# Halving the first batch's queries and giving every user of PSUM one bank, in an attention kernel followed by two matrix products

## The chip, the cores and the metric

The kernel runs on one core of one Trainium2 chip. The metric is the device time of one execution in microseconds (us), smaller is better. All executions quoted here are in the fast state, but for one of `e7_scores_apart`, which is left out of its figures. The medians are of the executions named beside them; an interval is a 95% interval of a ratio.

The engines are PE (the matmul engine, whose weight loads are listed apart as PEld), DVE and ACT (vector and scalar engine), POOL (permuting copies, and it issues the loads), SP (it issues transposes and stores) and 16 shared DMA engines. PSUM is the memory to which PE writes its results; it is handed out in banks. In these traces the engines keep to the program's order: two profiles of the changed kernel (the one below and `a0_changed_again`) have the same sequence on PE, DVE, ACT and POOL, 3584 matmuls on PE, though their waits differ by microseconds.

## The reference

```python
# q, k, v: (8, 12, 448, 64): batch, heads, sequence, head size
scores = q @ k.T / 8
e = exp(scores - max)
attn = (e / (sum(e) + exp(-max))) @ v              # "softmax off by one"
x = attn, heads side by side                       # (8*448, 768)
h = x @ w_in                                       # (3584, 2048)
g = (a0 + a1 h + a2 h^2 + a3 h^3) / (1 + |b0||h| + |b1|h^2 + 1e-6)
out = g @ w_out                                    # (3584, 768), float32
```

Below, "score pass" is a group of matmuls `k.q` and the exponential that ACT makes of it; "sums" are the softmax denominators (d) and the weighted values (u) of one unit of four heads; "products" are the matmuls of `x @ w_in`; "outputs" are those of `g @ w_out`. There are 8 batches of 3 units.

## The kernel before

The kernel is built by a small list scheduler: each operation has an engine, an estimated duration and dependencies, and a greedy loop decides in which order the engines get them. Only that order reaches the chip. Batch 0's q and k are transposed by PE, all others by DMA transposes, after POOL has permuted them into a single buffer (`qp`, `kp`):

```python
kp = ring("kp", 1, [P, 2, J, 2, D])
qt = ring("qt", NK, [128, 2, J, P])                # NK = 3; P = 112
sps = [ps.tile([128, 2, 512], F32, ...) for i in range(2)]   # scores, 2 x 2 PSUM banks
gen = [ps.tile([128, 2, 512], F32, ...) for i in range(2)]   # all others, 2 x 2 banks
# ... cut ...
            pm = plan.add("perm", Op(f"pm{name}{n}", "POOL", 1.1, [ld[n], hist(xps, n, 1)], ...))
            x = plan.add("x", Op(f"x{name}{n}", "SP", 0.1, [pm, hist(qk_free, n, NK)], emit_x))
# ... cut: emit_x is nc.sync.dma_start_transpose(out=qt[...], in_=qp[...]) ...
        if b == 0:
            transpose_by_pe(n)
        else:
            transpose_by_dma(n)
```

A unit's sums are queued between the next unit's score passes, in two portions; after batch 0's last unit they stand alone:

```python
    for n in range(NB):
        beats = attention(n)                       # 8 score passes
        for half in range(2):
            for s in beats[2 * half:2 * half + 2]:
                plan.add("att", s)
            if prev is not None:
                plan.add("att", prev[half])        # d, then u, of the unit before
        for s in beats[4:]:
            plan.add("att", s)
        prev = attend(n)
        if n == NQ - 1 or n == NB - 1:             # NQ = 3
            for op in prev:
                plan.add("att", op)
            prev = None
```

The products of two column blocks of 128 fill one double slot of `gen` and leave it by one cast 896 wide:

```python
                for c in range(f % 2 * NQ, f % 2 * NQ + NQ):
                    nc.tensor.matmul(out=gen[unit["slot"]][:, f // 2, 0:S],
                                     lhsT=w_in_sb[gi][...], rhs=x_sb[b % NX][:, c, :], ...)
```

The loads go out in this order: keys, queries and values of units 0 to 2, `w_in0`, unit 3, `w_in1`, `w_in2`, unit 4, `w_in3`, unit 5, `w_out0` to `w_out3`, then the later units.

The softmax here doesn't subtract the row's maximum and nothing guards it: scores larger than these inputs give would overflow.

## Time and profile before

| | before |
|---|---|
| median of the first three runs | 482.59 us (480.96 to 482.86) |
| span of the profiled run | 479.5 us |
| PE busy, by the page | 433.8 us (90%) |
| PE streaming, by count | 392 us (82%) |
| DVE busy, ACT busy | 335.0, 319.8 us |

"Streaming" is the measure that this document argues with. A busy PE is not a streaming PE: the same product matmul has a mean of 357 ns in the groups of the page, though 24 of them in a row pass in 4.65 us (0.194 us each) in the chain of waits. So I counted the matmuls that start in each 20 us and multiplied by what one costs in an undisturbed row: 0.194 us a product, 0.163 an output, 0.051 a sum, 0.10 a score matmul; one of half length counts half. The Trainium skill ("Perfetto Trace Analysis", Identifying the Most-Contended Engine) says likewise that the busy share of matmuls is not a good measure of how close a kernel is to its limit, because they are pipelined. It expects pipelined matmuls to look smaller in the trace; here they look larger (357 for 194 ns).

The page of the kernel before: its busy times, then the span in 40 slices of 12 us, one digit a slice in tenths, then the granted PE clock and the DMA engines.

```profile
span 479.5 us, 7892 instructions
PE 433.8 (90%) x3296; PEld 210.0 (44%) x3296; DVE 335.0 (70%) x389; ACT 319.8 (67%) x337; POOL 123.0 (26%) x186
PE   3873977897998999999999999999999999998985
DVE  1210579579796887738879976766879887899900
PEclk9997889799999999999999999999999999999999
DMA  9999998915685565528777537627031011111222
```

DVE is nearly idle in the first four slices (48 us): it has no products to cast. DMA stands at 8 or 9 tenths in the first eight. PE's waits lie in the same stretch. The timeline of PE of the kernel before, as start, duration, instructions, and in brackets the wait just before them and what ended it:

```profile
35.75 1.87 PE L417 MATMUL gen<-e,vn 112*32 112x448 f16 x32
...
45.68 1.00 PE L391 MATMUL sps<-qt,kt 64*112 64x448 f16 x4 [8.05 <-DMA qt<-qp]
46.61 1.30 PE L481 MATMUL gen<-x,w_in 128*128 128x448 f16 x3
...
63.60 0.58 PE L391 MATMUL sps<-qt,kt 64*112 64x448 f16 x4 [2.98 <-DMA qt<-qp]
...
457.13 11.87 PE L569 MATMUL gen<-w_out,g 128*128 128x384 f16 x72 [1.55 <-DVE g L519]
```

Batch 0's last sums end at 37.6 us. PE stands 8.05 us before the scores of batch 1, whose queries are still in a DMA transpose, and starts the first product only at 46.61 us. The chain of waits of the kernel before (start, duration, what ran) holds these transfers:

```profile
19.53 10.13 DMA w_in<-in_moe_w_in_dram
31.42 10.43 DMA kt<-kp
46.46 17.00 DMA qt<-qp
```

A transposition of queries takes 17.00 us here. The list of DMA issues gives, last on the line, the median over the whole run:

```profile
kt<-kp SPq DMA_TRANSPOSE x21, 3.4
qt<-qp SPq DMA_TRANSPOSE x21, 3.5
```

So one and the same transpose lands three to five times later in the head, beside the weight loads, than in steady state. The form-by-form groups of the kernel before (busy us, mean ns) show two costs that the change touches, the loading of keys into PE and the casts:

```profile
L391 PEld LDWEIGHTS <-kt 64*112 64x112 f16 x384 | 21.2, 130 | 62.8 <-issue 56.4 <-DMA kt<-kp 5.8 <-DVE kt L319 0.3
L498 DVE CAST h<-gen 128x896 f16<-128x896 f32 x60 | 64.9, 1086 | 49.5 <-PE gen L481 48.8 <-issue 0.3
```

### The profile page before, as it was taken

How to read it: one execution, taken by the hardware profiler on the slowest of the kernel's cores; microseconds unless marked ns; L12 is line 12 of the kernel's file. 1: busy time of each engine (PE TensorE's matmuls, PEld its weight loads, DVE VectorE, ACT ScalarE, POOL GpSimd, SP SyncE). 2: the span in 40 equal slices, each digit the busy share in tenths (PEclk: the TensorE clock that was granted, in tenths of full speed). 3: DMA queues.
4: the chain of work that ended last, by engine and by line, in shares of the span. 5: the costliest groups of instructions: out<-in, count | busy, mean ns of one | idle time of the engine just before them, and what ended most of it. 6: DMA issues, size and time to landing. Idle time of an engine off the chain costs nothing.

```text
span 479.5 us, 7892 instructions
## 1 busy us (share of the span) xinstructions
PE 433.8 (90%) x3296; PEld 210.0 (44%) x3296; DVE 335.0 (70%) x389; ACT 319.8 (67%) x337; POOL 123.0 (26%) x186
## 2 busy tenths in 40 slices
PE   3873977897998999999999999999999999998985
PEld 2421423343543444444444444444444445554553
DVE  1210579579796887738879976766879887899900
ACT  3792477867688586966869776876679782555611
POOL 6674135504540344033430432022000100010000
PEclk9997889799999999999999999999999999999999
DMA  9999998915685565528777537627031011111222
GB/s 127 183 202 190 202 163 120 128 24 87 95 99 108 91 96 98 103 32 119 116 125 109 77 78 126 105 58 101 31 72 35 0 34 34 33 34 33 68 66 67
DMA packets 82564, 43.98 MB, mean 92 GB/s; under 512 B 41568, under 2 KB 78944, under 8 KB 82528
## 3 DMA queue, kind: packets, MB, share of 16 engines
q0 software_dynamic: 38784, 22.81, 35.3%
q1 hardware_dynamic: 43744, 20.66, 20.9%
q8 instruction: 26, 0.43, 0.4%
q14 instruction: 10, 0.08, 0.1%
HBM read 45.62 MB, written 11.01 MB: 118 GB/s over the span
## 4 chain that ended last, share of the span: by engine, by line
PE 58%; DVE 15%; ACT 11%; DMA 10%; issue 4%; POOL 1%; DVEq 0%; POOLq 0%; ACTq 0%
PE gen L569 24%; PE gen L481 19%; PE gen L417 8%; PE sps L391 6%; ACT e L397 5%; DMA w_in<-in_moe_w_in_dram 4%; DMA qt<-qp 4%; DVE h L498 3%; DVE g L519 3%; DVE n L515 2%; ACT c L533 2%; DMA kt<-kp 2%; DVE n L519 2%; DVE c L519 2%; ACT c L530 1%
## 5 line engine op out<-in xcount | busy, mean ns | idle before, releaser
L397 ACT ACTIVATE e<-sps 112x896 f16<-112x896 f32 x192 | 166.5, 922 | 83.5 <-PE sps L391 82.9
L481 PE MATMUL gen<-x,w_in 128*128 128x448 f16 x768 | 161.3, 357 | 3.8 <-ACT o L579 1.5
L569 PE MATMUL gen<-w_out,g 128*128 128x384 f16 x768 | 134.2, 326 | 2.7 <-DVE g L519 2.3
L481 PEld LDWEIGHTS <-w_in 128*128 128x128 f16 x768 | 71.3, 98 | 83.4 <-issue 25.4
L498 DVE CAST h<-gen 128x896 f16<-128x896 f32 x60 | 64.9, 1086 | 49.5 <-PE gen L481 48.8
L569 PEld LDWEIGHTS <-g 128*128 128x128 f16 x768 | 72.2, 98 | 60.9 <-issue 12.0
L391 PE MATMUL sps<-qt,kt 64*112 64x448 f16 x384 | 65.0, 395 | 21.2 <-DMA qt<-qp 11.0
L530 ACT ACTIVATE c<-c,oneeps_c 128x1792 f16<-128x1792 f16 x32 | 57.4, 1794 | 36.2 <-DVE c L519 36.1
L519 DVE TENSOR_TENSOR n<-n,h 128x1792 f16<-128x1792 f16 x64 | 71.0, 1110 | 0.9
L552 POOL COPY gx<-g 128x1024 f16<-128x1024 f16 x8 | 9.3, 1158 | 198.2 <-DVE g L519 179.2
L533 ACT ACTIVATE c<-c 128x1792 f16<-128x1792 f16 x32 | 54.5, 1702 | 0.3
L438 DVE TENSOR_TENSOR x<-gen,lden 128x896 f16<-128x896 f32 x24 | 26.1, 1086 | 35.7 <-PE gen L417 35.7
L345 POOL COPY kp<-kn 112x256 uint32<-112x256 uint32 x42 | 24.8, 620 | 101.1 <-DMA kt<-kp 96.3
L519 DVE TENSOR_TENSOR g<-n,c 128x1792 f16<-128x1792 f16 x32 | 35.0, 1095 | 21.2 <-ACT c L533 20.5
L391 PEld LDWEIGHTS <-kt 64*112 64x112 f16 x384 | 21.2, 130 | 62.8 <-issue 56.4
L515 DVE TENSOR_SCALAR n<-n,abc 128x1792 f16<-128x1792 f16 x64 | 45.2, 706 | 1.2
L417 PE MATMUL gen<-e,vn 112*32 112x448 f16 x768 | 43.1, 368 | 1.0 <-ACT lden L430 0.9
L579 ACT ACTIVATE o<-gen 128x768 f32<-128x768 f32 x28 | 22.7, 810 | 25.6 <-PE gen L569 25.6
L519 DVE TENSOR_TENSOR c<-c,w 128x1792 f16<-128x1792 f16 x32 | 35.2, 1100 | 0.0
L345 POOL COPY qp<-qn 112x256 uint32<-112x256 uint32 x42 | 27.6, 686 | 14.7 <-DMA qt<-qp 12.2
L417 PEld LDWEIGHTS <-vn 112*32 112x32 f16 x768 | 20.0, 99 | 21.6 <-issue 11.0
L417 PE MATMUL gen<-e,ones 112*32 112x448 f16 x384 | 24.9, 379 | 3.6 <-DVE h L498 3.2
(32 smaller groups left out, 230.7 us busy)
## 6 DMA issues: line engine op xcount, KB each, us to landing
kn<-in_k_dram POOLq DMA_DIRECT2D x24, 224.0 KB, 4.2
qn<-in_q_dram POOLq DMA_DIRECT2D x24, 224.0 KB, 5.0
vn<-in_v_dram POOLq DMA_DIRECT2D x24, 224.0 KB, 6.2
w_in<-in_moe_w_in_dram POOLq DMA_DIRECT2D x12, 256.0 KB, 10.1
w_out<-in_moe_w_out_dram POOLq DMA_DIRECT2D x4, 768.0 KB, 20.1
out_dram<-o SPq DMA_DIRECT2D x8, 336.0 KB, 3.0
out_dram<-o SPq DMA_DIRECT2D x8, 288.0 KB, 2.8
out_dram<-o SPq DMA_DIRECT2D x8, 240.0 KB, 2.6
```

The costliest lines, as they stand in the source:

```text
L345: nc.gpsimd.tensor_copy(out=mid[0].bitcast(U32)[:, pr], in_=src[n % NN].bitcast(U32)[:, 2 * pr:2 * pr + 2] .rearrange("p e j d -> p j e d"))
L391: nc.tensor.matmul(out=sps[m % NS][0:P, hh, 0:S], lhsT=kt[n % NK][r, pr, j, :], rhs=qt[n % NK][r, pr].rearrange("p j c -> p (j c)"), start ...
L397: nc.scalar.activation(out=e_sb[m % NE], in_=sps[m % NS][0:P, :, 0:S], func=AF.Exp, scale=scale)
L417: nc.tensor.matmul(out=gen[unit["slot"]][32 * i:32 * i + 32, half, 0:S], lhsT=lhs(i, j), rhs=e_sb[m % NE][:, i % 2, :], start=(j == 0), st ...
L438: nc.vector.tensor_tensor(out=x_sb[b % NX][:, 2 * qd:2 * qd + 2, :], in0=gen[un_u["slot"]][:, :, 0:S], in1=r, op=ALU.mult)
L481: nc.tensor.matmul(out=gen[unit["slot"]][:, f // 2, 0:S], lhsT=w_in_sb[gi][:, c // 2, c % 2, (fc % FG) * 128:(fc % FG + 1) * 128], rhs=x_s ...
L498: nc.vector.tensor_copy(out=dst, in_=src)
L515: return lambda: nc.vector.tensor_scalar(out=out, in0=in0, scalar1=s1, scalar2=s2, op0=op0, **kw)
L519: return lambda: nc.vector.tensor_tensor(out=out, in0=in0, in1=in1, op=ALU.mult)
L530: lambda: nc.scalar.activation(out=c, in_=c, func=AF.Ln, bias=oneeps_c)))
L533: lambda: nc.scalar.activation(out=c, in_=c, func=AF.Exp, scale=-1.0)))
L569: nc.tensor.matmul(out=gen[unit["slot"]][:, nh, 0:HD], lhsT=lhs, rhs=w_out_sb[f // 2][:, fc % FG, nh * HD:(nh + 1) * HD], start=(fc == 0), ...
```

## The change

The intent has four parts and a consequence.

1. *Halves.* Batch 0's attention runs for 224 query columns first and for the other 224 after. The products of the first half can start when half of the exponentials are made.
2. *Single banks.* The four banks of `gen` are handed out singly. A cast is 448 wide instead of 896, so a bank comes free sooner; casts, multiplications and output copies double in number.
3. *Joining.* A unit's sums (d and both u) are queued in one block behind the first two score passes of the next unit. The scheduler opens a unit only when three banks are free.
4. *Padding.* The keys' buffer is 16 columns longer and 128 columns are loaded as weights.
5. The queue of POOL is reordered: permutations go ahead of loads, `w_in1` ahead of unit 3, and with that `w_out1` to `w_out3` end up behind a permutation.

The diff holds more than this intent: one more buffer each for transposed q and k (NK) and for `h` (NH), and other durations and tie-breaks in the scheduler. In what follows they belong to "the other parts".

The core of the diff, with cuts:

```diff
-    NE, NX, NV, NN, NK, NH, NO, NS = 12, 3, 5, 2, 3, 2, 3, 2
+    NE, NX, NV, NN, NK, NH, NO, NS = 12, 3, 5, 2, 4, 3, 3, 2
-    qt = ring("qt", NK, [128, 2, J, P])
-    kt = ring("kt", NK, [128, 2, J, P])
+    qt = ring("qt", NK, [128, 2 * S])
+    kt = ring("kt", NK, [128, 2 * S + 16])
-    gen = [ps.tile([128, 2, 512], F32, name=f"gen{i}") for i in range(2)]
+    NGEN = 4
+    gen = [ps.tile([128, 512], F32, name=f"gen{i}") for i in range(NGEN)]
-        "POOL": ("load",  "perm", "gx"),
+        "POOL": ("perm", "load", "gx"),
+    units = [(0, qd, q0, S // 2) for q0 in (0, S // 2) for qd in range(NQ)]
+    units += [(b, qd, 0, S) for b in range(1, B) for qd in range(NQ)]
 # ... cut: in the scheduler
+            if name in ("att", "e"):
+                late = op.due > t
+                if op.opens:
+                    banks = self.bank_times()
+                    late |= len(banks) < 3 or banks[1][0] > t or banks[2][0] > t + 1.2
+                if late:
+                    rank = 9
 # ... cut: a score pass
-                            out=sps[m % NS][0:P, hh, 0:S], lhsT=kt[n % NK][r, pr, j, :],
+                                out=sps[m % NS][:, hh, ci * qw:(ci + 1) * qw],
+                                lhsT=kt[n % NK][r, c0:c0 + 128],
 # ... cut: a product and its cast
-            src = gen[unit["slot"]][:, :, 0:S]
+            src = gen[unit["bank"]][:, 0:S]
 # ... cut: the loads
-    w_in_ops = [w_in_op(0)]
+    w_in_ops = [w_in_op(0), w_in_op(1)]
     loads(3)
-    w_in_ops.append(w_in_op(1))
     w_in_ops.append(w_in_op(2))
 # ... cut: the attention queue
+    for i in range(len(units)):
+        passes = scores(i)
+        for s in passes[:2]:
+            plan.add("att", s)
+        for op in prev or []:
+            plan.add("att", op)
+        for s in passes[2:]:
+            plan.add("att", s)
+        prev = attend(i, m0)
 # ... cut: the products
+    for un in range(8):
+        slots.append((un, gemm1, (0, 0, S // 2, un)))
+        slots.append((8 + un, gemm1, (0, S // 2, S // 2, un)))
```

## The prediction

> **What bounds the kernel now.** Busy time (page, part 1): PE 434 of 479.5 us, DVE 335, ACT 320. Real streaming: the chain of waits shows 24 product matmuls in 4.65 us, 20 output matmuls in 3.36, 32 attention matmuls in 1.63, two of a score pass in 0.20. That is 0.194, 0.163, 0.051 and 0.10 us each; over 768, 896, 1152 and 384 of them about 396 us, so 84 are lost. Matmuls counted in 20 us stretches say where: 0 to 120 us holds 65 us of streaming (loss 55); 120 to 460 holds 319 of 340 (loss 21); after 460 about 5.
>
> The head: the chain runs through w_in DMAs (11.6 to 29.7 us), the first transposed keys (kt, 31.4 to 41.8) and queries (qt, 46.5 to 63.5). Such a transpose lands in 3.5 us in steady state (DMA view); here it takes 10 to 17 beside weight loads. PE, in order, stands before these scores, starts products only at 46.6 us, and is cold (granted 0.54 in 40 to 50). DVE's first cast comes at 52 us; then DVE holds PE back (100% busy at 80 to 90): two double slots serve all users.
>
> **What the change does.**
> - Batch 0 in query halves: products need half as many exponentials. At 0.81 us each, the first half's x is ready near 25 us; products fill the second half's ACT-bound attention, and DVE starts about 20 us earlier. Cost: 288 more, shorter matmuls, perhaps 2 us.
> - DMA order: w_out1 to w_out3 move behind the second permutation pair; w_in1 moves ahead of batch 1's first loads. I expect the first kt/qt at 38 and 42 us (before 41.8, 45.7), the second qt near 50 (63.5), the third near 62 (70.6).
> - Four single banks: DVE casts 60 to 120, multiplications 24 to 54, output copies 28 to 56. A 896-wide cast repeats each 1.00 us[...]: DVE +6 us, ACT +5; neither bounds. A bank frees after about 0.55 instead of 1.0 us.
> - PE block switches: 277 before, 306 after by instruction order; at about 0.1 us, +3 us. Score weights 64x112 load in 123 ns, 128-wide ones in 98 (medians). The Trainium skill ("TensorE: Matmul & The Clock Gate", Weight-path perf modes) says fast load needs 128 columns; the trace agrees in direction. Mostly hidden: at most 3 us gained.
>
> **Critical path and time.** By 65 us I expect 45 us of streaming done, a point before reached near 93. Remaining 353 us, with 4% loss (6% before; banks free sooner, a third h buffer) 14 us; tail 5; timed minus span 3. Sum 65+353+14+5+3 = 440.
>
> Predicted **441 us, range 430 to 456** (before 482.6). Chances: faster by over 2% 0.95, within 2% 0.04, slower 0.01. The gain is nearly all in the first 120 us.
>
> **What would show it.** First product matmul near 25 us (46.6); first cast near 27 (52); streaming in 0 to 120 us of 85 to 95; clock near 1.0 in 40 to 60; PE waiting for kt/qt under 10 us (17 before); from 120 us on, 19.2 or more per 20 us; kt weight loads near 98 ns; DVE 341 to 345, ACT about 325.
>
> **What would make it wrong.** If DMA, saturated to 63 us, still lands batch 1's transposes late, PE idles at 30 to 60 and half the head gain goes (455). If attention, taking three of four banks at once, starves the products, or in-order DVE and ACT delay short casts, the steady loss stays 6% or more (450). If it nearly vanishes, 430.

## The result

| | before | changed |
|---|---|---|
| median | 482.68 us (480.96 to 482.86, 4 runs) | 466.15 us (465.89 to 470.43, 4 runs) |
| span of the profiled run | 479.5 us | 468.7 us |
| first product | 46.61 us | 28.98 us |
| PE streaming by 60, 80, 100, 120 us | 23.2, 36.8, 48.2, 63.8 us | 23.6, 37.3, 48.1, 66.5 us |
| streaming from 120 to 420 us | 277.5 us | 288.6 us |

The ratio is 0.969 (0.963 to 0.975): faster by 3%, where I had predicted 441 us, and outside the range. Ratios here are the mean time of one kernel's fast runs over that of the other's of the same rounds, so not quite the ratio of the medians quoted. The profiled run of the changed kernel is the slowest of its four (470.43 us; the spans of the other three are 464.1 to 464.6 us).

The page of the changed kernel, the same lines:

```profile
span 468.7 us, 8639 instructions
PE 427.1 (91%) x3584; PEld 219.3 (47%) x3584; DVE 345.1 (74%) x483; ACT 324.1 (69%) x375; POOL 116.0 (25%) x186
PE   3874879689999899999999999999999999999695
DVE  1321849967969997769898887689797998999700
PEclk9997879979999999999999999999999999999999
DMA  9999999979855198309881988328311011102122
```

DVE begins earlier (8 tenths in the fifth slice, where it had 5), and DMA is still full in the first ten slices but one. The timeline of PE of the changed kernel:

```profile
28.98 0.75 PE L482 MATMUL gen<-x,w_in 128*128 128x224 f16 x6
...
44.26 0.93 PE L388 MATMUL sps<-qt,kt 64*128 64x448 f16 x4 [6.36 <-DMA qt<-qp]
45.12 0.94 PE L420 MATMUL gen<-e,ones 112*32 112x224 f16 x16
...
62.00 0.93 PE L388 MATMUL sps<-qt,kt 64*128 64x448 f16 x4 [4.94 <-DMA qt<-qp]
...
442.95 15.51 PE L576 MATMUL gen<-w_out,g 128*128 128x384 f16 x84 [4.63 <-DVE g L523]
```

The first product comes 17.6 us earlier, as intended. But PE still stands 6.36 us for the queries, now with the sums of batch 0 (45.12 us) waiting behind those scores, and 4.94 us for the second queries. The chain of waits of the changed kernel names the transposes again, and the list of DMA issues shows longer medians over the whole run:

```profile
30.31 13.81 DMA qt<-qp
62.69 14.40 DMA qt<-qp
```

```profile
kt<-kp SPq DMA_TRANSPOSE x21, 5.2
qt<-qp SPq DMA_TRANSPOSE x21, 6.2
```

The form-by-form groups, and PE's waits for transposed queries in the summary of waits (us in total, times, longest):

```profile
L388 PEld LDWEIGHTS <-kt 64*128 64x128 f16 x432 | 15.6, 96 | 57.6 <-issue 56.5
L499 DVE CAST h<-gen 128x448 f16<-128x448 f32 x120 | 73.8, 619 | 34.3 <-PE gen L482 34.0
```

```profile
PE sps L388 <- DMA qt<-qp: 13.6, 4, 6.4
```

*Where the 10.8 us between the two profiled spans come from*, by streaming counts: 2.7 us in the first 120 us; 2.5 from 120 to 180; 8.6 from 180 to 420; then 3.0 are given back after 420 us, where PE waits 4.63 us for DVE's last `g`. The head, from which nearly all of the gain was to come, gained little, although its first product came 17.6 us sooner. (In the second profile of the same kernel, `a0_changed_again`, it gained 4.3.)

### The profile page after: what moved, and what is told of

It reads as the page before. It is cut to its first block, busy times and chain, and to the rows that moved or that the text cites. A ratio compares the mean times of both kernels' runs of the same rounds, so it can differ in the third digit from the quotient of the medians.

```text
span 468.7 us, 8639 instructions
## 1 busy us (share of the span) xinstructions
PE 427.1 (91%) x3584; PEld 219.3 (47%) x3584; DVE 345.1 (74%) x483; ACT 324.1 (69%) x375; POOL 116.0 (25%) x186
## 4 chain that ended last, share of the span: by engine, by line
PE 63%; DVE 16%; DMA 9%; ACT 5%; issue 5%; POOL 2%; SPq 0%; DVEq 0%; POOLq 0%; ACTq 0%
PE gen L576 25%; PE gen L482 22%; PE gen L420 8%; PE sps L388 7%; DMA qt<-qp 6%; DVE n L523 3%; DVE n L519 3%; DVE h L499 3%; DMA qn<-in_q_dram 2%; ACT e L395 2%; DVE c L523 2%; DVE g L523 2%; DVE c L519 2%; DVE w L519 1%; ACT c L537 1%
## 5 line engine op out<-in xcount | busy, mean ns | idle before, releaser
L482 PE MATMUL gen<-x,w_in 128*128 128x448 f16 (+1 forms) x864 | 163.6, 337 | 0.3 <-DVE x L447 0.3
L482 PEld LDWEIGHTS <-w_in 128*128 128x128 f16 x864 | 81.4, 99 | 70.9 <-issue 17.1
L499 DVE CAST h<-gen 128x448 f16<-128x448 f32 x120 | 73.8, 619 | 34.3 <-PE gen L482 34.0
L388 PE MATMUL sps<-qt,kt 64*128 64x448 f16 (+1 forms) x432 | 59.8, 349 | 21.6 <-DMA qt<-qp 13.6
L447 DVE TENSOR_TENSOR x<-gen,lden 128x448 f16<-128x448 f32 (+1 forms) x54 | 28.6, 566 | 40.0 <-ACT lden L435 32.9
L590 ACT ACTIVATE o<-gen 128x384 f32<-128x384 f32 x56 | 27.2, 487 | 34.8 <-PE gen L576 34.7
L420 PE MATMUL gen<-e,vn 112*32 112x448 f16 (+1 forms) x864 | 44.1, 350 | 0.0
L388 PEld LDWEIGHTS <-kt 64*128 64x128 f16 x432 | 15.6, 96 | 57.6 <-issue 56.5
L354 POOL COPY kp<-kn 112x256 uint32<-112x256 uint32 x42 | 23.2, 583 | 60.5 <-DMA kt<-kp 51.3
L354 POOL COPY qp<-qn 112x256 uint32<-112x256 uint32 x42 | 23.2, 581 | 23.3 <-DMA qt<-qp 22.9
L283 POOL DMA_DIRECT2D vn<-in_v_dram x24 | 17.2, 718 | 41.5 <-PE sps L388 23.6
```

Source lines behind the costliest of these rows:

```text
L354: nc.gpsimd.tensor_copy(out=mid[0].bitcast(U32)[:, pr], in_=src[n % NN].bitcast(U32)[:, 2 * pr:2 * pr + 2] .rearrange("p e j d -> p j e d"))
L388: nc.tensor.matmul(out=sps[m % NS][:, hh, ci * qw:(ci + 1) * qw], lhsT=kt[n % NK][r, c0:c0 + 128], rhs=qt[n % NK][r, pr * S + q0:pr * S + ...
L420: nc.tensor.matmul(out=gen[unit["bank"]][32 * h:32 * h + 32, 0:qw], lhsT=lhs(h, j), rhs=e_sb[m % NE][:, h % 2, c0:c0 + qw], start=(j == 0) ...
L447: mult.emit = lambda s=s, uu=uu: nc.vector.tensor_tensor(out=x_sb[b % NX][:, 2 * qd + s, q0:q0 + qw], in0=gen[uu["bank"]][:, 0:qw], in1=ld ...
L482: nc.tensor.matmul(out=gen[unit["bank"]][:, fi * qw:(fi + 1) * qw], lhsT=w_in_sb[wg][:, c // 2, c % 2, (fc % FG) * 128:(fc % FG + 1) * 128 ...
L499: nc.vector.tensor_copy(out=dst, in_=src)
```

## The experiments

**Theories.** (A) The DMA transposes of batch 1 land 10 to 17 us after issue whatever the order of the loads; PE, in order, stands before the scores that need them. (B) The head is bound by the bytes to be loaded, wherever they are placed. (C) The order of PE's instructions and the pace of the exponentials bound the head, not DMA. Three more were tested: (D) it is the new place of the `w_out` loads, which collide with those transposes; (E) the joined blocks and the single banks cost in steady state what the head gained; (F) the halves themselves are worth little.

Every short diff below is against the changed kernel unless said otherwise. Every kernel gave the reference's result but one (`e3_w_out_quarter`), which is wrong. The time of the kernel before for each call: 481.68 us in the first, 481.83 in the second, 482.93 in the third, 483.22 in the fourth. The calls ran on three different chips, so a difference of 2 or 3 us between runs of different calls is not clear of noise.

### First call: which part of the head

**e1_pe_transposes.** PE transposes batch 1 too, and no DMA transpose (nor its permutation) is left in the first 60 us.

```diff
-        (transpose_by_pe if n < NQ else transpose_by_dma)(n)
+        (transpose_by_pe if n < 2 * NQ else transpose_by_dma)(n)
```

> The changed kernel with batch 1's queries and keys transposed on PE, as batch 0's are, so that no DMA transpose runs beside the weight loads (all other data as before). Theory A (the head is lost to DMA transposes that take 10 to 17 us each beside the w_out loads, and PE stands in order before their scores): PE's waits for qt (13.6 us) go, x of batch 1 is ready 10 us or more earlier, time 453 to 460 us (466 without the edit). Theory B (the head is bound by the bytes to be loaded, the q, k, v and weight loads land late whatever is done with them): the waits move to the loads of q and k, time 464 to 467. Theory C (the order of PE's instructions and the pace of the exponentials bound it, not DMA): 464 to 468.

Measured: 451.72 us (451.42 to 453.13), ratio 0.936 (0.931 to 0.942). Streaming by 60, 80, 100, 120 us: 31.9, 47.1, 63.7, 82.4 us, where the changed kernel had 23.6, 37.3, 48.1, 66.5. The scores of batch 1 start without a wait for DMA, and the longest wait left after the first loads is at the end, for DVE's last `g`; both in its timeline of PE:

```profile
39.10 0.36 PE L388 MATMUL sps<-qt,kt 64*128 64x448 f16 x2
...
425.27 3.06 PE L576 MATMUL gen<-w_out,g 128*128 128x384 f16 x9 [4.69 <-DVE g L523]
```

This run favours theory A, beyond its own forecast of 453 to 460: 14.4 us hang on how batch 1 is transposed. Theory C, which expected no gain, falls.

**e2_w_out_later.** Unit 6's loads go ahead of all `w_out`.

```diff
+    loads(6)
     w_out_ops = [w_out_op(cg) for cg in range(NG)]
-    for n in range(2 * NQ, NQ * B):
+    for n in range(2 * NQ + 1, NQ * B):
```

> The changed kernel with the four w_out loads issued after the loads of the seventh unit of four heads instead of before them. Theory A: the second qt, 17.0 us from issue to landing with w_out beside it, lands in about 6 to 9 us; its scores start near 53 instead of 62 us; time 458 to 462. Theory B: bytes are only reordered, what is gained before 60 us is lost when the first output products wait for w_out near 82; time 464 to 468. Theory C: 465 to 467.

Measured: 463.24 us, ratio 0.961 (0.956 to 0.966). The second queries land in 9.5 us (16.9 in the changed kernel), but the third take 19.15 us, as its chain of waits shows:

```profile
51.29 19.15 DMA qt<-qp
```

The place of `w_out` is worth some 3 us, not clear of noise. So theory D falls as the main cause: the slowness moves from one transpose to another.

**e3_w_out_quarter.** The `w_out` loads bring a quarter of their bytes; the result is wrong (relative error 1.76).

```diff
-                out=w_out_sb[cg],
-                in_=moe_w_out[cg * CW:(cg + 1) * CW].rearrange("(c p) f -> p c f", p=128))
+                out=w_out_sb[cg][:, 0],
+                in_=moe_w_out[cg * CW:cg * CW + 128])
 # ... cut: the output products
-                        rhs=w_out_sb[f][:, fc % FG, nh * HD:(nh + 1) * HD],
+                        rhs=w_out_sb[f][:, 0, nh * HD:(nh + 1) * HD],
```

> Wrong result on purpose: each w_out load brings one of its four chunks, and the output products read that chunk four times; the instruction order on every engine is the same. 2.3 MB of about 14 MB written by DMA in the first 94 us go. Theory A: the second and third qt land in 6 to 9 us instead of 14 to 17: 455 to 460 us. Theory B: at about 170 KB per us 13 us of DMA time go and the head shortens by nearly as much: 453 to 457. Theory C: 464 to 467. Its use beside the run with w_out later: if this one gains and that one doesn't, volume decides, not place.

Measured: 463.74 us (460.95 to 464.65), ratio 0.961 (0.955 to 0.966). The first two pairs of transposes land as late as ever (keys 9.6 and 10.9 us, queries 13.8 and 14.3); only the third queries are quick (7.5). Theory B falls as the main cause: with three quarters of those bytes gone, 2 to 3 us come back of the 25 that were missing. Theory A's forecast for this run (455 to 460, with quick second and third queries) missed too: the transposes stay slow beside the loads that are left.

**e4_batch0_whole.** Batch 0 whole, the rest of the change kept.

```diff
-    units = [(0, qd, q0, S // 2) for q0 in (0, S // 2) for qd in range(NQ)]
+    units = [(0, qd, 0, S) for qd in range(NQ)]
 # ... cut
-    for un in range(8):
-        slots.append((un, gemm1, (0, 0, S // 2, un)))
-        slots.append((8 + un, gemm1, (0, S // 2, S // 2, un)))
-    for b in range(1, B):
+    for b in range(B):
```

> The changed kernel with batch 0 in one piece, not in query halves; everything else (single banks, padding, joined blocks, DMA order rule) stays. My prediction held that halving brings most of the gain: then 476 to 481 us. The profile after says the head gained nothing (67 us of streaming by 120 us against 65): then within 1% of the changed kernel, 463 to 469, with the first product matmul later (35 us or more instead of 29) and the same third qt near 77 us.

Measured: 481.39 us (479.0 to 482.78), ratio 0.998 (0.992 to 1.003): the same as the kernel before. So theory F falls: the halves are worth 15 us, and all other parts of the change together nothing. Its timeline of PE shows one reason:

```profile
41.85 0.93 PE L388 MATMUL sps<-qt,kt 64*128 64x448 f16 x4 [4.12 <-DMA qt<-qp]
42.72 1.69 PE L420 MATMUL gen<-e,ones 112*32 112x448 f16 x16
```

The sums of batch 0's last unit run at 42.72 us, behind scores that wait for a transpose; the kernel before ran them at 34.5 to 37.6 us. Joining a unit's sums to the next unit's scores ties batch 0 to batch 1's transposes.

Streaming counts place the loss and the gain. At 180 us the kernel before has done 117.4 us of streaming, this one 111.8, the changed one 122.6. From 180 to 420 us they do 223.9, 232.6 and 232.5. So the parts other than the halves cost 5.6 us early and gain 8.7 later; the halves gain 10.8 early.

### Second call: the parts of the steady state

**a0_changed_again.** The changed kernel unedited, for comparison within the call.

> The changed kernel itself, unedited, on the chip of the three runs beside it, so that effects under 1% can be read: 464 to 468 us, ratio 0.966 to 0.970.

Measured: 466.61 us (465.6 to 468.9), ratio 0.967 (0.964 to 0.971).

**e5_keys_112.** The padding undone.

```diff
-                                out=sps[m % NS][:, hh, ci * qw:(ci + 1) * qw],
-                                lhsT=kt[n % NK][r, c0:c0 + 128],
+                                out=sps[m % NS][0:P, hh, ci * qw:(ci + 1) * qw],
+                                lhsT=kt[n % NK][r, c0:c0 + P],
```

> Padding undone alone: score weights 64x112 again, same instruction order on every engine. In the traces between 130 and 370 us the mean cost of a score block above its streaming is 0.152 us before and 0.117 after, and there are about 110 such blocks in all: if that difference is the padding's, 3 us slower than the changed kernel run beside it (0.4 to 0.9%), and kt weight loads of 123 instead of 96 ns. If the weight loads are hidden, within 0.2%.

Measured: 470.17 us, ratio 0.975 (0.971 to 0.978). The padding is worth 3.6 us. The mean key load goes from 96 ns back to 136 (the kernel before: 130), in its form-by-form groups:

```profile
L388 PEld LDWEIGHTS <-kt 64*112 64x112 f16 x432 | 23.9, 136 | 49.2 <-issue 48.5
```

In 130 to 370 us a block of score matmuls that had no wait took, from its first start to the start of what follows, 0.087 us more than its streaming in the changed kernel, 0.120 in this one and 0.124 in the kernel before (means of 64, 64 and 56 blocks; the expectation's figures are 0.03 higher by another count, with the same difference). Over the changed kernel's 107 score blocks 0.033 us each make 3.5 us. The Trainium skill ("TensorE: Matmul & The Clock Gate", Weight-path perf modes) says that weights of 128 columns have a fast load; the trace agrees in direction, with 96 for 130 ns, 1.4 times, where the page has about twice.

**e7_scores_apart.** The sums in two portions again, d behind two score passes and u behind four.

```diff
-        for op in prev or []:
+        for op in (prev or [])[:1]:
+            plan.add("att", op)
+        for s in passes[2:4]:
+            plan.add("att", s)
+        for op in (prev or [])[1:]:
             plan.add("att", op)
-        for s in passes[2:]:
+        for s in passes[4:]:
```

> The joining undone alone: two score passes stand between a unit's sums and its products again, as before the change. 270 changes between kinds of matmul on PE instead of 231: at about 0.1 us each 4 us slower than the changed kernel (0.5 to 1.2%). If a change costs nothing on the critical path, within 0.3%; the scheduler may also reorder more than I expect, then up to 2% either way.

Measured: 469.41 us in the median of its five fast executions (467.75 to 473.6; a sixth, of 474.98, counts as slow), ratio 0.975 (0.971 to 0.980). Joining is worth about 3 us (2.8 by these medians), in a kernel whose own executions spread over 6 us: PE changes between kinds of matmuls 231 times in the changed kernel and 270 times here (237 in the kernel before; products and outputs are one kind here). So theory E falls for the joining; the padding (e5) gains too, 3 to 4 us. For the single banks theory E was not tested.

**e6_three_banks.** One single bank less.

```diff
-    NGEN = 4
+    NGEN = 3
```

> Three single banks instead of four. If the finer release of banks is what holds PE at 98% in steady state, one bank less makes it wait for casts and output copies and the kernel is 1.5 to 5% slower than the changed one. If banks are not short, within 0.5% (fewer changes of kind, 136 instead of 231, might then even gain 1%).

Measured: 541.66 us, ratio 1.123 (1.119 to 1.127), a far larger loss than I expected. The summary of waits of this kernel says what happens:

```profile
PE sps L388 <- ACT e L395: 48.8, 90, 2.6
```

The scheduler opens a unit only with three banks free, which are then all banks: nothing else is held at that time, and score passes then run alone at the pace of the exponentials. PE waits 48.8 us for them in 90 waits, and the clock granted falls to 0.896. The order of instructions is a different one too (136 changes of kind instead of 231), so this is no measure of one bank's worth; it shows that the condition `opens` and the number of banks belong together.

### Third call: without the head's transposes, and towards a better version

**e8_two_mid.** Two buffers for the permuted q and k, so that a permutation does not wait for the transpose before it.

```diff
-    qp = ring("qp", 1, [P, 2, J, 2, D])
-    kp = ring("kp", 1, [P, 2, J, 2, D])
+    qp = ring("qp", 2, [P, 2, J, 2, D])
+    kp = ring("kp", 2, [P, 2, J, 2, D])
 # ... cut: mid[0] becomes mid[n % 2], hist(xps, n, 1) becomes hist(xps, n, 2)
```

> Two buffers instead of one for the permuted keys and queries that the DMA transposes read, all else as changed. What makes the transposes of batch 1 late is either (S) the chain through the single buffer: the next permutation waits until the transpose before has landed; then the second and third kt and qt are issued 4 to 12 us earlier, and the time falls to 455 to 461; or (L) the slow landing itself, 12 to 17 us each beside the loads on the queues: issued earlier they share the same engines and land hardly earlier: 464 to 468.

Measured: 464.69 us (462.75 to 468.15), ratio 0.962 (0.956 to 0.969), about 2 us better, not clear of noise. The third transpose of queries is issued at 49.55 us instead of 62.69, but takes 18.85 us instead of 14.40:

```profile
49.55 18.85 DMA qt<-qp
```

Issued 13.1 us sooner, it lands 8.7 us sooner (68.4 instead of 77.1 us). The six transposes now take 9.6 to 18.9 us each. So the single buffer is a small part of theory A too; the larger part is the transfer itself, beside the loads.

**c4_pe_transposes_whole.** The edits of e1 and e4 together: batch 0 whole, batch 1 transposed by PE.

> Batch 1 transposed on PE and batch 0 in one piece. With DMA transposes halving was worth 15 us (466 against 481). If halving works as I predicted, by giving PE and DVE work during batch 0's attention, it is worth about as much here too: 462 to 468 against 451.7 with halves. If halving only covered the waits for late transposes, this lies within 4 us of 451.7.

Measured: 466.08 us, ratio 0.964 (0.959 to 0.970). Against e1 (0.936) the halves are worth 14 us, against e4 (0.998) the PE transposes 15 us. The two add up; neither eats the other.

**c2_pe_transposes_act_casts.** The edit of e1, and all casts of the last batch on ACT, for the wait at the end.

```diff
-        on_act = b == B - 1 and un % 2 == 1
+        on_act = b == B - 1
-        (transpose_by_pe if n < NQ else transpose_by_dma)(n)
+        (transpose_by_pe if n < 2 * NQ else transpose_by_dma)(n)
```

> Batch 1 transposed on PE, and all 16 casts of the last batch on ACT instead of every second one. With PE transposes PE waits 4.7 us at the end for the last g while DVE is 98% busy and ACT about 60%. Eight casts of 0.62 us leave DVE: if DVE's load sets the tail, 446 to 449 us; if the last group's own chain does, 451 to 452.

Measured: 444.98 us (444.58 to 445.4), ratio 0.921 (0.915 to 0.927). It beats both kernels, with a correct result: 21 us less than the changed one. The wait for the last `g` falls from 4.69 us (e1) to 1.53, in its timeline of PE:

```profile
418.92 13.82 PE L576 MATMUL gen<-w_out,g 128*128 128x384 f16 x84 [1.53 <-DVE g L523]
```

In the last batch DVE was busy 9.7 of 10 while ACT was near 60%; eight casts moved from one to the other gave 6.7 us.

**c3_pe_transposes_w_out_later.** The edits of c2 and e2 together.

> The same with the w_out loads moved behind the loads of the seventh unit. In the changed kernel those keys took 30 us from issue to landing behind w_out and the first scores of batch 2 waited until 89 us; with PE transposes the DMA transposes of batch 2 begin at 61.7 us. If they still hold PE back between 70 and 100 us, 2 to 4 us less than the run without this edit; if the output products then wait for w_out instead, the same or up to 3 us more.

Measured: 446.52 us (444.92 to 450.74), ratio 0.925 (0.919 to 0.932): no gain over c2. Once no transpose stands in the head, the place of `w_out` no longer matters.

The streaming counts of the kernels that matter, in us done by the given time:

| by | 60 | 80 | 100 | 120 | 180 | 420 us | the end |
|---|---|---|---|---|---|---|---|
| before | 23.2 | 36.8 | 48.2 | 63.8 | 117.4 | 341.3 | 392.2 |
| changed | 23.6 | 37.3 | 48.1 | 66.5 | 122.6 | 355.1 | 392.2 |
| e4, batch 0 whole | 18.8 | 30.7 | 45.8 | 59.2 | 111.8 | 344.4 | 392.2 |
| e1, PE transposes | 31.9 | 47.1 | 63.7 | 82.4 | 138.6 | 373.0 | 392.2 |
| c4, e1 and e4 | 29.7 | 45.8 | 56.1 | 75.7 | 126.9 | 360.7 | 392.2 |
| c2, e1 and casts on ACT | 32.8 | 47.9 | 66.7 | 85.7 | 141.7 | 374.4 | 392.2 |

The lead of e1 over the changed kernel is made between 40 and 100 us (15.6 us at 100 us) and kept to 180 (16.0); of that 14.4 us remain in the total. The lead of the halved over the whole batch 0 is made by 180 us: 10.8 us (changed and e4) and 11.7 (e1 and c4).

### Fourth call: the joined sums of batch 0

What was then open: whether the joining of batch 0's last sums, and not only the transposes, took part of the head's gain; and whether the kernel before would have gained as much from PE transposes.

**e10_own_block.** The sums of batch 0's last half unit are queued by themselves, before batch 1's first scores, as the kernel before did it.

```diff
         prev = attend(i, m0)
+        if i == 2 * NQ - 1:
+            for op in prev:
+                plan.add("att", op)
+            prev = None
```

> The changed kernel with the sums and products of batch 0's last unit put straight after its own scores, as the kernel before had it, instead of after the first score passes of batch 1. In the changed kernel PE stands 6.4 us before those passes (until 44.26 us) with the sums' inputs ready. If joining costs the head that: 462 to 465 us, the last products of batch 0 attended near 40 instead of 47 us. If the time is set by the later waits for qt all the same: 465 to 467.

Measured: 463.7 us (462.32 to 465.27), ratio 0.959 (0.953 to 0.965), some 2.5 us better than the changed kernel, not clear of noise.

**e11_whole_own_block.** The same with batch 0 whole (e4, with the new lines at `i == NQ - 1`).

> Batch 0 in one piece (481.4 us, the same as the kernel before) with the same edit. There the whole last unit of batch 0, 2.4 us of PE work that every product waits for, stood behind the qt wait until 41.85 us, and x of batch 0 was ready near 47 instead of 38 us as in the kernel before. If this is what ate the steady gain of the other parts, 474 to 478; if not, 480 to 482.

Measured: 475.14 us, ratio 0.984 (0.979 to 0.990), where e4 had 0.998. So 6 of the microseconds that the other parts gained were lost at this one place when batch 0 is whole, and some 2.5 when it is in halves. With the sums by themselves the halves are worth 11.4 us (475.14 against 463.7).

**c5_best_own_block.** The edits of c2 and e10 together.

> The best version so far (PE transposes for batch 1, casts of the last batch on ACT, 445.0 us) with the same edit. There no score waits for qt at that place, so nothing stands behind it: 443 to 447.

Measured: 453.7 us (453.27 to 454.16), ratio 0.939 (0.935 to 0.944): 8.7 us slower than c2, against my expectation. The scheduler found another order, and its timeline of PE has from 70.90 to 78.42 us nothing but score passes, 0.8 us apart:

```profile
73.90 0.56 PE L388 MATMUL sps<-qt,kt 64*128 64x448 f16 x2 [2.45 <-ACT e L395]
74.71 0.56 PE L388 MATMUL sps<-qt,kt 64*128 64x448 f16 x2 [0.25 <-ACT e L395]
```

The granted clock of 60 to 80 us is 0.84, and 11.8 us of streaming are done there (15.1 in c2). A local improvement can cost more in a greedy order than it gains; why the greedy loop chose so was not followed up.

**b1_before_pe_transposes.** The edit of e1 in the kernel before.

```diff
-        if b == 0:
+        if n < 2 * NQ:
             transpose_by_pe(n)
 # ... cut
-                ready = qk_ready[n][pr if b == 0 else 0]
+                ready = qk_ready[n][pr if n < 2 * NQ else 0]
```

> The kernel before with only batch 1 transposed on PE. In the changed kernel this edit is worth 14 to 15 us with and without halves. If the late DMA transposes hold up the kernel before as well, 468 to 475; if its batch 0 products, which run in that time, hide them, 480 to 483.

Measured: 474.83 us (472.1 to 478.61), ratio 0.983 (0.976 to 0.991). The waits for queries vanish and the first product comes at 40.02 us instead of 46.61. The transposes cost the kernel before 8 us and the changed one 14 to 15: the earlier the products could start, the more there is to lose by standing before a score.

## Why the prediction was wrong

**The step that failed.** "I expect the first kt/qt at 38 and 42 us (before 41.8, 45.7), the second qt near 50 (63.5), the third near 62 (70.6)", and from it "By 65 us I expect 45 us of streaming done". The first pair came nearly as expected, keys at 38.9 and queries at 44.1 us; the second queries landed at 61.9 us, 12 late, and the third at 77.1, 15 late. I had read 10 to 17 us as the cost of a collision with particular weight loads, which the new order would avoid. The runs show it with every order of loads that was tried: with `w_out` later (e2), with three quarters of it gone (e3), with transposes issued earlier (e8), most of the first six stay slow, at 9 to 19 us.

**What stands in its place.** The sum was 65 + 353 + 14 + 5 + 3 = 440. In the profiled run the 45 us of streaming were reached at 91.3 us, where the kernel before reached them at 96.9 (93 by the prediction's count). The term that was mis-sized is thus the first: 91.3 for 65, which is 26.3 of the 30 us by which the profiled run (470.43) exceeds the sum. The other terms were off too, and partly cancel: 347 us of streaming were left, where 353 had been counted (the prediction's 396 in all takes 3.36 / 20 = 0.168 us an output and not the 0.163 that it names); 30.2 us were lost after that point and not 14 + 5 (7.2 before 120 us, 11.4 from 120 to 420, 11.6 after); timed minus span was 1.7 and not 3. In e1, which has no DMA transposes in the head, the first term is 76.6, 14.7 less, and the time is 14.4 less. So of the 26.3 us, 14.7 hang on the transposes. The other 11.6 are, as far as the trace shows, the pace of the head even then: the first product at 28.98 us and not 25, a block of six half-length products taking 0.68 us from its start to the next block's (28.98 to 29.66 us) where 6 x 0.097 = 0.58 was counted, and the second half's exponentials between the blocks. I have not split these 11.6 further.

**Point by point.**

- *"Batch 0 in query halves"*: right in mechanism and about right in size. The halves are worth 15 us (e4), 14 without DMA transposes (c4 and e1), 11 with the sums by themselves (e10 and e11). The first product came at 28.98 us, predicted near 25; the first cast at 32.50, predicted near 27, before 52.22.
- *"the kernel's head"*: streaming in 0 to 120 us was predicted 85 to 95 us. It was 66.5; with PE transposes 82.4 (e1) and 85.7 (c2). PE waited 13.6 us for queries, predicted under 10.
- *Clock*: predicted near 1.0 in 40 to 60 us, it was 0.74, and 0.51 from 40 to 50, after PE stood 6.36 us. The Trainium skill ("TensorE: Matmul & The Clock Gate", What's actually happening) says that PE falls to half its clock after an idle window of about 3.4 us, and the trace agrees that such a wait brings half the clock, though here it came 2.4 us after the last matmul's end (37.90 us): the clock records show half from 40.26 to 50.49 and from 60.73 to 67.56 us. So a wait costs more than its length: after the first two waits for queries PE worked 11.8 us at half clock (44.26 to 50.49 and 62.00 to 67.56) and did 6.0 us of streaming in them, an estimate of 6 us lost beside the waits themselves. In e1 the clock is full from 23.41 to 81.44 us. It differs between executions: in `a0_changed_again` the mean of 40 to 60 us is 0.90.
- *From 120 us on*: right, if only just. 19.2 or more per 20 us was predicted; the mean to 420 us was 19.24 (18.5 in the kernel before). This is where the change's time came from in the end: 11.1 us in this stretch, padding (3.6 in all, e5) and joining (about 3 in all, e7) among it. The prediction had called padding "Mostly hidden: at most 3 us gained" and counted block switches as a cost of 3 us, 277 before and 306 after. Counted its way, with products and outputs as two kinds, the traces show 276 and 305, as predicted; without these changes they are 237 and 231. What single banks are worth alone was not measured; e6 does not tell it.
- *The tail*: predicted 5 us lost; 11.6 were, after 420 us, against 8.6 in the kernel before, because the last batch is bound by DVE (c2: casts moved off DVE gave 6.7 us).
- *Unforeseen*: joining sends batch 0's last sums behind a score that waits for DMA (e11: 6 us; e10: 2.5 us, not clear of noise). And the keys of unit 6 landed 30.4 us after their issue (47.2 to 77.6 us), behind `w_out1` to `w_out3`, while POOL waited 9.17 us for them; the prediction had named that order only as a relief for transposes. e2 gives its worth, about 3 us, not clear of noise.
- *DVE and ACT*: 341 to 345 and about 325 us predicted, 345.1 and 324.1 measured. Key loads: a median near 98 ns predicted, 93 measured (mean 96).
- *"What would make it wrong"* had the cause in its first sentence, with 455 us for half of the head's gain. In streaming by 120 us all but 2.7 us of it was gone.

With the transposes off the head and the casts off DVE's tail (c2), 445 us were measured, 4 above the prediction of 441.

**What stays open.** Why a transpose is that slow beside loads was not isolated: e1 shows what leaving the DMA path is worth, and the landings show that slowness goes with loads in flight, but no run had transposes in the head and no loads. e1 also frees POOL of twelve permuting copies; e8 says that waiting for the permutation buffer is a small part. The worths of 2 to 3 us read from e2, e3, e8 and e10 are not clear of noise: the intervals of their ratios overlap with that of `a0_changed_again` (0.964 to 0.971). What the single banks, the extra buffers and the scheduler's new figures are worth alone was not run. A change of one part also moves the greedy order, as c5 and e6 show, so the single worths (15, 3, 3.6, 2.5 us) need not add up exactly.

## What to carry to other kernels

An earlier start of work is worth its time only as far as the in-order engine is not stopped behind something else: before counting a head's gain, list what the engine meets next and when the data of that lands, taking landing times from the same stage of the trace and not from the median of the run. A transfer that was slow beside heavy loads will most likely be slow again after the loads are reordered; take it off the DMA engines (here 14 us), or do not let finished work be queued behind it. Count streaming in stretches of time, and remove one part at a time: here the halves, the padding and the joining gained, the waits for transposes and batch 0's joined sums lost, and the total alone told none of it.

## What the Trainium skill lacked or had wrong

- "DMA: Bandwidth & Descriptors", Rules for kernel authors: "A transpose next to ordinary DMAs needs nothing" holds for the result. As to time, the page gives the bandwidth of a transpose (Latency and other measured facts: 261 GB/s or more), but no page says what it takes beside loads. Here a transpose of 224 KB whose median is 3.4 to 3.5 us over the run of the kernel before took 10 to 17 us beside loads in five of batch 1's six (all six in the changed kernel), and up to 19 in e2. The section Queues, rings and completion order says that a DMA engine takes packets from its queues in turn, which would fit; no run here isolates it.
- The same page, Anatomy of one DMA, fits one load as 2.0 us + bytes/436e3. For a piece of `w_in` (256 rows of 512 values, 256 KB in half precision at the destination) that is an estimate of 2.6 us (3.2 with the 512 KB of float32 at the source); the list of DMA issues of the kernel before gives a median of 10.1 us for the twelve of them, and in the changed kernel the keys of unit 6 took 30.4 us behind `w_out`. The page gives no figure for a load that waits behind others.
- "TensorE: Matmul & The Clock Gate", LDWEIGHTS, gives columns/1.2 ns: 93 ns for 112 columns, 107 for 128, 27 for 32. The traces show medians of 123 (112 columns, kernel before), 93 (128, changed kernel) and 97 (32, both). The order is the other way for 112 and 128, which the fast load of the next point would explain; and 32 columns cost as much as 128.
- The same page, Weight-path perf modes, gives the fast load of 128 columns but not what padding to it is worth when loads mostly overlap matmuls: 3.6 of 470 us here (e5).
